# Eight experts in another order: all moved up by one position where neighbours had changed places

## The chip, the cores and the metric

One core of a Trainium2 chip runs the whole program in one launch. The metric is the time of one execution in device microseconds (us), lower is better. The engines are TensorE (PE in the views; PEld is its weight load, which overlaps), VectorE (DVE), ScalarE (ACT), GpSimd (POOL) and SyncE (SP, which here only issues transfers).

## What is computed

Attention with a compressive memory feeds a mixture of experts with one expert per token. There are 2304 tokens of 512 features, 8 experts, and 1024 hidden features in each.

```python
logits = x @ w_gate
expert_idx = np.argmax(logits, axis=1)
...
for e in range(E):
    mask = expert_idx == e
    ...
    h = np.maximum(xe @ w1[e], 0.0)
    ye = h @ w2[e]
    out[mask] = gate_w[mask, None] * ye
```

The inputs come from a seeded generator, so the routing is fixed. It gives experts 0 to 7 these numbers of tokens: 2, 465, 120, 834, 36, 680, 12, 155.

## The kernel before

The first 262 us are the attention stage, with its steps placed by a table of times (`K`), and at its end the routing: each token's expert, its rank within it, and the table `idx` of the tokens in the order in which they are to be worked on. The rest is the expert stage, which this change is about.

The experts are worked on one after another in eight **positions**. `weight_unit` (line 78) says which expert's weights stand at position p: p ^ 1, so 1, 0, 3, 2, 5, 4, 7, 6. `setup` (lines 184 to 186) puts the gate's columns into the same order, so that column p of the logits is that of position p. `Routing.consts` (line 1029) writes the weights `w8` by which a tie goes to the lower expert.

The tokens of a position are cut into blocks of 128. A remainder of 65 to 127 makes one more full block, a remainder of up to 64 a half block (lines 1167 to 1176: counts + 127 and + 63, shifted by 7). The counts reach every engine through the tile `r_cnt` at run time, so each engine runs loops and branches over them (`conv_loops` for ScalarE and VectorE, `turns` for SP, blocks F, H, X, Y, N, Z for TensorE). The first block is done ahead of the loops by straight code; blocks are counted here from that one as 0.

A block on TensorE: 96 products that make the hidden features (line 1581, into `ph`), then the second products into `py` (line 1597 for a full block, line 1594 for a half one, in two column halves). VectorE turns `ph` into `hT` in two parts, hi and lo (lines 1750, 1752). ScalarE moves `py` to `ysb` (lines 1710, 1708), and GpSimd scatters the rows to the output (line 1503). For the next block, GpSimd gathers 128 rows (line 1489), VectorE multiplies them with their gate values into `xn` (lines 1779, 1782), SP issues two transposes into `xB` (line 1410), and VectorE copies that to `xT` (line 1793), which TensorE's next block waits for.

Weights come as fp32, eight units of 512 KB for each position. SP loads them four units (a half) at a time, one half in each turn (line 1383). ScalarE makes the hi part of a unit (line 1271, `conv_hi`), VectorE the lo part (line 1275, `conv_lo`); one half is converted in each block until all are done, halves 0 to 13 for positions 1 to 7. At position e, `conv_loops` first finishes the halves of position e + 1 and then goes on with those of e + 2. Every combination is a copy of the body of its own in the program: `step(e, 0, ...)` for full, `step(e, 1, ...)` for half blocks. In a full block's body VectorE's order is hT of the first half, one conversion, hT of the second half, one conversion, the copy to xT, two conversions. In a half block's body it is both hT, one conversion, the copy to xT, three conversions (`cuts`).

TensorE has three copies of each body, because three sets of converted weights take turns; they stand in the program in this order, each followed by its branches:

```python
for i in range(3):
    with block(f"F{i}"):
        pe_body(rr, i, 0)
...
    with block(f"H{i}"):
        pe_body(rr, i, 1)
```

Position p uses copy p mod 3: F for its full blocks, H for its half block. From F0 the program goes to F0 again (more full blocks), to H0, to F1 or to H1 (line 1656).

Of the kernel before, what the change touches and what calls it, by code (L numbers as in the profile page):

```python
# [76 lines left out]

def weight_unit(w1, w2, p, u):

    e = p ^ 1  # L80
    if u < 4:
        return w1[e, 128 * u:128 * u + 128, :]
    return w2[e, 256 * (u - 4):256 * (u - 4) + 256, :].rearrange("(f p) d -> p f d", p=128)
# [18 lines left out]
def attention(nc, tc, es, q, k, v, M_prev, z_prev, beta, wg, w1, w2, x_dram, logits, mem, rout=None):  # L102
# [44 lines left out]
    for ab in range(2):  # L147
        nc.gpsimd.affine_select(out=maskt[64 * ab:64 * ab + 64], in_=maskt[64 * ab:64 * ab + 64],
                                pattern=[[-1, 64]], compare_op=ALU.is_ge, fill=-1e30, base=0,
                                channel_multiplier=1)  # L150
# [21 lines left out]
    def setup():  # L172
        wg_sb = const.tile([128, 4, 8], F32, name="wg_sb")
        nc.sync.dma_start(out=wg_sb, in_=wg.rearrange("(c p) e -> p c e", p=128))
        bt = const.tile([128, 8], F32, name="bt")
        nc.sync.dma_start(out=bt, in_=beta.rearrange("(o h) -> o h", o=1).to_broadcast([128, 8]))

        gm = const.tile([128, 8], F32, name="gm")
        gl = const.tile([128, 8], F32, name="gl")
        nc.scalar.activation(out=bt, in_=bt, func=AF.Tanh, scale=0.5)  # L180
        nc.vector.tensor_scalar(out=gm, in0=bt, scalar1=0.5 * SX, scalar2=0.5 * SX, op0=ALU.mult, op1=ALU.add)
        nc.vector.tensor_scalar(out=gl, in0=bt, scalar1=-0.5 * SX, scalar2=0.5 * SX, op0=ALU.mult, op1=ALU.add)

        wg_in, wg_sb = wg_sb, const.tile([128, 4, 8], F32, name="wg_sw")
        for i in range(2):
            nc.vector.tensor_copy(out=wg_sb[:, :, i::2], in_=wg_in[:, :, 1 - i::2])
        IW = const.tile([128, 4, 2, 72], F32, name="IW")
        nc.gpsimd.memset(IW, 0.0)
        for hh in range(2):
            r = slice(64 * hh, 64 * hh + 64)  # L190
            nc.vector.tensor_copy(out=IW[r, :, hh, 0:64], in_=ident[r, 64 * hh:64 * hh + 64].unsqueeze(1).to_broadcast([64, 4, 64]))
            nc.vector.tensor_copy(out=IW[r, :, hh, 64:72], in_=wg_sb[r])
        mz = xp.tile([128, 32, 64], F32, tag="xb", name="mz")
        early = xp.tile([128, 512], F32, tag="xt", name="early")
        zt = early[0:32, 256:384].rearrange("p (a d) -> p a d", a=2)
        for hh in range(2):
            nc.sync.dma_start(out=zt[:, hh], in_=z_prev.rearrange("b h d -> (b h) d"))
        mh = const.tile([128, 32, 73], F16, name="mh")
        ml = const.tile([128, 32, 73], F16, name="ml")
        nc.gpsimd.memset(ml[64:128], 0.0)  # L200
        T["gm"] = gm
        mw = early[:, 0:256].rearrange("p (i e) -> p i e", e=8)
        wgp = early[:, 384:512].rearrange("p (c m) -> p c m", c=4)
        nc.gpsimd.memset(wgp, 0.0)
        for hh in range(2):
            nc.vector.tensor_copy(out=wgp[64 * hh:64 * hh + 64, :, 8 * hh:8 * hh + 8], in_=wg_sb[64 * hh:64 * hh + 64])
        mt = xp.tile([128, 32, 64], F32, tag="xb", name="mt2").rearrange("p a d -> p (a d)")
        T.update(IW=IW, gl=gl, mh=mh, ml=ml, mz=mz, mw=mw, zt=zt, wgp=wgp, pws=mt[:, 1024:1536].rearrange("p (b a d) -> p b a d", b=4, a=2),
                 mt=mt[:, 0:1024].rearrange("p (c b d) -> p c b d", c=4, b=4))
# [578 lines left out]
    def wload(e, u):  # L788
        nc.sync.dma_start(out=as_unit(wplace(e, u), u), in_=weight_unit(w1, w2, e, u))
# [116 lines left out]
    at(K["k1"], load, 1, "k")  # L906
    at(K["k1"], load, 1, "q")
    at(K["setup"], setup)
    at(K["v1"], load, 1, "v")
    for i in range(4):  # L910
# [68 lines left out]
NE = 8  # L979
# [9 lines left out]
class Routing:  # L989
# [25 lines left out]
    def consts(s):  # L1015
        V, G, kp = s.nc.vector, s.nc.gpsimd, s.tc.keep_in_program_order
        kp(G.memset(s.tri, 1.0))
        kp(G.affine_select(out=s.tri, in_=s.tri, pattern=[[1, 128]], compare_op=ALU.is_gt, fill=0.0, base=0, channel_multiplier=-1))
        kp(G.memset(s.ones, 1.0))
        kp(G.memset(s.cnt[:, NE:], 0))  # L1020
        kp(G.memset(s.idx[:, NS:NS + 1], 2303))
        kp(G.memset(s.ids[:, NS:NS + 1], 2304))
        ii = s.idx[:, 0:NS]
        it = s.tmp
        kp(G.iota(ii, pattern=[[128, NS]], base=0, channel_multiplier=0))
        kp(V.tensor_scalar(out=s.col, in0=ii, scalar1=BIG, scalar2=None, op0=ALU.add))
        kp(G.iota(it, pattern=[[-1, 128]], base=0, channel_multiplier=0))
        kp(V.tensor_copy(out=s.neg, in_=it))
        kp(G.iota(it[:, 0:NE].rearrange("p (a b) -> p a b", b=2), pattern=[[-2, NE // 2], [1, 2]], base=NE - 1, channel_multiplier=0))
        kp(V.tensor_copy(out=s.w8, in_=it[:, 0:NE]))  # L1030
        kp(G.iota(it[:, NE:2 * NE], pattern=[[128 * NJ, NE]], base=0, channel_multiplier=0))
        kp(V.memset(s.first, 0.0))
        kp(V.memset(s.less, 0.0))
        kp(V.memset(s.less[0:1, 0:1], -128.0))
        kp(V.tensor_copy(out=s.first[0:1], in_=it[0:1, NE:2 * NE]))
        tok = it[:, 16:34]
        for i in range(2):
            kp(G.iota(tok[:, 9 * i:9 * i + 8].rearrange("p (b t) -> p b t", t=4), pattern=[[576, 2], [128, 4]], base=1152 * i - 2304,
                      channel_multiplier=1))
            for a in range(2):  # L1040
                kp(G.iota(tok[64 * a:64 * a + 64, 9 * i + 8:9 * i + 9], pattern=[[0, 1]], base=512 + 576 * (2 * i + a) - 2304, channel_multiplier=1))
        kp(V.tensor_copy(out=s.vals, in_=tok))
# [181 lines left out]
def experts(nc, tc, es, x_dram, mem, rout, w1, w2, out):  # L1224
# [29 lines left out]
    with tc.tile_critical():  # L1254
# [127 lines left out]
        def load(e, u):  # L1382
            SP.dma_start(out=as_unit(stage[e % 2][u], u), in_=weight_unit(w1, w2, e, u)).then_inc(wsem[e % 2][u], 16)
# [457 lines left out]
```

## Time and profile before

| | us |
|---|---|
| median of three runs | 503.66 |
| lowest, highest | 499.33, 504.02 |
| profiled execution, its own time | 500.64 |
| its span, first to last instruction | 498.9 |
| TensorE busy | 462.2 |
| VectorE busy | 356.3 |
| ScalarE busy | 221.7 |
| GpSimd busy | 212.6 |

The mean granted clock of TensorE over the span is 0.98 of full speed. The span and all rows below are of that one profiled execution; its own time is the span and 1.7 us around it. In a row of a timeline, the first figure is the start in us from the span's start, the second the length; a bracket gives the engine's idle time just ahead of it and what ended it. "issue" stands for idle time that ended with nothing the profile shows.

### The profile page before, as it was taken

How to read it: one execution, taken by the hardware profiler on the slowest of the kernel's cores; microseconds unless marked ns; L12 is line 12 of the kernel's file. 1: busy time of each engine (PE TensorE's matmuls, PEld its weight loads, DVE VectorE, ACT ScalarE, POOL GpSimd, SP SyncE). 2: the span in 40 equal slices, each digit the busy share in tenths (PEclk: the TensorE clock that was granted, in tenths of full speed). 3: DMA queues.
4: the chain of work that ended last, by engine and by line, in shares of the span. 5: the costliest groups of instructions: out<-in, count | busy, mean ns of one | idle time of the engine just before them, and what ended most of it. 6: DMA issues, size and time to landing. Idle time of an engine off the chain costs nothing.

```text
span 498.9 us, 14292 instructions
## 1 busy us (share of the span) xinstructions
PE 462.2 (93%) x5269; PEld 316.8 (64%) x5270; DVE 356.3 (71%) x785; ACT 221.7 (44%) x361; POOL 212.6 (43%) x395
## 2 busy tenths in 40 slices
PE   2999799999999989999989996999999999999795
PEld 0555356566666646657656774966777667777774
DVE  2788489787869647999885776898844588743682
ACT  3688465556666564557510443433300333300611
POOL 6567558367748344656231421232232122231132
PEclk9999799999999999999979999899999999999998
DMA  5567979899898989866148999799873459952332
GB/s 118 126 119 159 181 153 163 177 192 232 176 163 163 270 166 184 180 167 218 47 133 286 245 286 281 227 268 333 272 149 97 125 158 346 292 132 76 57 76 70
DMA packets 170106, 90.57 MB, mean 182 GB/s; under 512 B 151471, under 2 KB 152751, under 8 KB 170032
## 3 DMA queue, kind: packets, MB, share of 16 engines
q1 hardware_dynamic: 166192, 77.95, 67.2%
q0 software_dynamic: 3840, 11.80, 7.8%
q8 instruction: 26, 0.43, 0.4%
q14 instruction: 48, 0.39, 0.3%
HBM read 55.35 MB, written 11.60 MB: 134 GB/s over the span
## 4 chain that ended last, share of the span: by engine, by line
PE 60%; DVE 12%; DMA 10%; SPq 8%; issue 5%; ACT 2%; POOL 2%; DVEq 1%; POOLq 0%; ACTq 0%
PE m_ph L1581 17%; PE m_py L1597 13%; PE o L565 7%; PE st L491 5%; DMA m_xB<-m_xn 4%; SPq L275 3%; PE sm L596 3%; PE loc L677 3%; DMA m_xg<-x_scratch,m_ig 2%; PE sn L404 2%; SPq L277 2%; DMA QT<-mem 1%; PE m_py L1594 1%; PE wm L882 1%; DMA mem<-in_v_dram 1%
## 5 line engine op out<-in xcount | busy, mean ns | idle before, releaser
L1581 PE MATMUL m_ph<-m_xT,mem 128*128 128x128 f16 (+1 forms) x1344 | 68.8, 214 | 8.3 <-issue 4.3
L1581 PEld LDWEIGHTS m_ph<-m_xT,mem 128*128 128x128 f16 x1344 | 67.5, 100 | 12.2 <-issue 9.8
L412 DVE TENSOR_REDUCE mt<-sn 128x1 f32<-128x512 f32 (+4 forms) x83 | 54.4, 665 | 13.0 <-PE sn L410 10.7
L510 ACT ACTIVATE aT<-st 128x512 f32<-128x512 f32 x96 | 55.4, 594 | 18.4 <-PE st L491 18.0
L1710 ACT ACTIVATE m_y<-m_py 128x512 f32<-128x512 f32 x17 | 10.2, 597 | 117.0 <-PE m_py L1597 117.0
L495 POOL TENSOR_SCALAR_AFFINE_SELECT aT<-aT 128x128 f32<-128x128 f32 (+2 forms) x160 | 48.4, 320 | 32.3 <-ACT aT L510 30.3
L565 PE MATMUL o<-aT,mem 128*64 128x320 f32 (+4 forms) x320 | 59.2, 433 | 0.0
L1597 PE MATMUL m_py<-mem,m_hT 128*128 128x512 f16 x264 | 58.9, 379 | 0.0
L1750 DVE TENSOR_SCALAR m_hT<-m_ph 128x512 f16<-128x512 f32 (+1 forms) x46 | 29.0, 631 | 40.2 <-PE m_ph L1581 37.8
L1537 POOL COPY m_ig<-r_idx 128x1 int32 x22 | 4.1, 186 | 115.3 <-DVE m_xn L1782 114.3
L491 PE MATMUL st<-mem 128*128 128x64 f16 (+6 forms) x224 | 46.6, 262 | 0.4 <-ACT aL L532 0.2
L491 PEld LDWEIGHTS <-mem 128*128 128x128 f16 (+1 forms) x448 | 33.0, 99 | 16.3 <-issue 4.6
L1597 PEld LDWEIGHTS m_py<-mem,m_hT 128*128 128x128 f16 x264 | 25.3, 98 | 28.3
L491 PE MATMUL st<-QT,mem 66*128 66x64 f16 (+6 forms) x224 | 42.2, 262 | 0.4 <-ACT QT L455 0.4
L1581 PEld LDWEIGHTS m_ph<-m_xT,m_w 128*128 128x128 f16 x768 | 40.9, 98 | 1.8 <-issue 0.4
L1581 PE MATMUL m_ph<-m_xT,m_w 128*128 128x128 f16 (+1 forms) x768 | 41.6, 216 | 0.0
L1597 PE MATMUL m_py<-m_w,m_hT 128*128 128x512 f16 x168 | 37.4, 379 | 0.0
L565 PEld LDWEIGHTS o<-aT,mem 128*64 128x64 f32 x320 | 25.3, 137 | 16.7 <-issue 9.8
L1503 POOL DMA_INDIRECT out_dram<-m_y,m_is x23 | 25.5, 1109 | 20.1 <-POOL m_is L1509 18.0
L404 PE MATMUL sn<-mem 128*128 128x128 f16 (+3 forms) x158 | 31.4, 277 | 1.5 <-DVE mt L412 1.1
L1489 POOL DMA_INDIRECT m_xg<-x_scratch,m_ig x22 | 24.0, 1090 | 17.5 <-POOL m_ig L1537 17.5
L1275 DVE SCALAR_TENSOR_TENSOR mem<-mem,mem 128x1024 f16<-128x1024 f32 x24 | 28.6, 1218 | 2.5 <-ACT mem L1271 2.5
(257 smaller groups left out, 910.3 us busy)
## 6 DMA issues: line engine op xcount, KB each, us to landing
mem<-in_moe_w_dram SPq DMA_DIRECT2D x40, 512.0 KB, 6.0
m_stage<-in_moe_w_dram SPq DMA_DIRECT2D x24, 512.0 KB, 6.6
mem<-in_k_dram SPq DMA_DIRECT2D x32, 128.0 KB, 3.0
mem<-in_q_dram SPq DMA_DIRECT2D x32, 128.0 KB, 2.8
mem<-in_v_dram SPq DMA_DIRECT2D x32, 128.0 KB, 2.7
x_scratch<-xb SPq DMA_DIRECT2D x3, 1152.0 KB, 5.6
mem<-mem SPq DMA_DIRECT2D x6, 288.0 KB, 4.2
x_scratch<-xb SPq DMA_DIRECT2D x1, 864.0 KB, 3.8
```

Of the source, the lines that this page charges most:

```text
L404: nc.tensor.matmul(ps[:, c:c + k1 - k0], QT[:, 5 * hh + t, :], keys(hh)[:, k0:k1], start=(c == 0), stop=(k1 == parts[-1][3] and hh == part ...
L412: nc.vector.reduce_max(out, v, axis=AX.X)
L491: nc.tensor.matmul(ps[:, c:c + n], kk[:, kb, :], qq[:, w:w + n], start=(first and i == 0 and j == 0), stop=(last and i == 1 and j == len(p ...
L495: nc.gpsimd.affine_select(out=ap, in_=ap, pattern=pattern, compare_op=ALU.is_ge, fill=0.0, base=base, channel_multiplier=-1)
L510: nc.scalar.activation(out=a, in_=ps, func=AF.Exp, scale=ESC)
L565: nc.tensor.matmul(o[64 * hh:64 * hh + 64, q0:q0 + n], vv, aa, start=(j == 0), stop=(j == 4), skip_group_check=True)
L1275: V.scalar_tensor_tensor(out=W[e % 3][1][:, u], in0=stage[e % 2][u], scalar=SW, in1=W[e % 3][0][:, u], op0=ALU.mult, op1=ALU.subtract).the ...
L1489: G.indirect_dma_start(out=x.rearrange("p h e -> p (h e)"), out_offset=None, in_=x_dram, in_offset=bass.IndirectOffsetOnAxis(ap=i, axis=0) ...
L1503: G.indirect_dma_start(out=out, out_offset=bass.IndirectOffsetOnAxis(ap=i, axis=0), in_=ysb[:, j], in_offset=None, bounds_check=bound, oob ...
L1581: mm = PE.matmul(ph[i2][:, f, 0:N], w[:, kc, c:c + 128], x[:, j, kc, 0:N], start=(i == 0), stop=(i == 11), skip_group_check=True)
L1597: mm = PE.matmul(py, hh, ww[:, 4 + ff // 2, c:c + 512], start=st, stop=sp_)
L1750: V.tensor_scalar(out=hT[i2][0][:, :, 0:N], in0=ph[i2][:, :, 0:N], scalar1=0.0, scalar2=None, op0=ALU.max).then_inc(S[hi], 1)
```

## The change

Position p gets expert (p + 1) mod 8, so the order is 1, 2, 3, 4, 5, 6, 7, 0. The gate's columns and the tie weights follow. No loop, no body and no queue is touched.

```diff
 def weight_unit(w1, w2, p, u):
 
-    e = p ^ 1
+    e = (p + 1) % 8
...
         wg_in, wg_sb = wg_sb, const.tile([128, 4, 8], F32, name="wg_sw")
-        for i in range(2):
-            nc.vector.tensor_copy(out=wg_sb[:, :, i::2], in_=wg_in[:, :, 1 - i::2])
+        nc.vector.tensor_copy(out=wg_sb[:, :, 0:7], in_=wg_in[:, :, 1:8])
+        nc.vector.tensor_copy(out=wg_sb[:, :, 7], in_=wg_in[:, :, 0])
...
-        kp(G.iota(it[:, 0:NE].rearrange("p (a b) -> p a b", b=2), pattern=[[-2, NE // 2], [1, 2]], base=NE - 1, channel_multiplier=0))
+        kp(G.iota(it[:, 0:NE], pattern=[[-1, NE]], base=NE - 1, channel_multiplier=0))
+        kp(G.iota(it[:, NE - 1:NE], pattern=[[0, 1]], base=NE, channel_multiplier=0))
         kp(V.tensor_copy(out=s.w8, in_=it[:, 0:NE]))
```

What the counts make of it (F a full block, H a half one; position 0 has one more block ahead of the loops):

| position | expert before | tokens | blocks | expert after | tokens | blocks |
|---|---|---|---|---|---|---|
| 0 | 1 | 465 | FFF | 1 | 465 | FFF |
| 1 | 0 | 2 | H | 2 | 120 | F |
| 2 | 3 | 834 | 7 F | 3 | 834 | 7 F |
| 3 | 2 | 120 | F | 4 | 36 | H |
| 4 | 5 | 680 | 5 F, H | 5 | 680 | 5 F, H |
| 5 | 4 | 36 | H | 6 | 12 | H |
| 6 | 7 | 155 | F, H | 7 | 155 | F, H |
| 7 | 6 | 12 | H | 0 | 2 | H |

The bodies stand in the program as before, on every engine; the counts send the engines into others. On TensorE, these are the full body F0 and its branches, and behind it the half body H0, as they stand in the program before (`m_ph` the first products, `m_py` the second, `mem` the converted weights).

```order
L1581 MATMUL m_ph_4111<-m_xT,mem_59 128x128 x48
...
L1597 MATMUL m_py<-mem_59,m_hT_4098 128x512 x8
...
L1682 COMPARE_AND_BRANCH
L1684 COMPARE_AND_BRANCH
...
L1656 UNCONDITIONAL_BRANCH
L1581 MATMUL m_ph_4111<-m_xT,mem_59 128x64 x48
...
L1594 MATMUL m_py<-mem_59,m_hT_4098 64x256 x16
```

Position 3 ran the first of these two and now runs the second; position 1 ran H1 and now runs F1, their copies two bodies further on. So the way through the bodies was F0, H1, F2, F0, F1 and is F0, F1, F2, H0, F1.

On VectorE, at position 1, this is the step that ran before: the half body with the conversions of one half of weights, from behind the branch at line 1348 (`m_w` the converted weights of position 2, `m_stage` the loaded ones).

```order
L1779 TENSOR_SCALAR m_xn_4094<-m_xg_4093 128x512
L1782 SCALAR_TENSOR_TENSOR m_xn_4095<-m_xg_4093,m_xn_4094 128x512
L1750 TENSOR_SCALAR m_hT_4098<-m_ph_4111 128x4x64
...
L1752 SCALAR_TENSOR_TENSOR m_hT_4101<-m_ph_4112,m_hT_4100 128x4x64
L1275 SCALAR_TENSOR_TENSOR m_w_4089<-m_stage_4102,m_w_4089 128x1024
L1793 COPY m_xT<-m_xB 128x1024
L1275 SCALAR_TENSOR_TENSOR m_w_4089<-m_stage_4102,m_w_4089 128x1024 x3
```

In its place the full body with the same four conversions runs, which stands directly behind the branch at line 1343; this is its second part in the program before.

```order
L1750 TENSOR_SCALAR m_hT_4100<-m_ph_4112 128x512
L1752 SCALAR_TENSOR_TENSOR m_hT_4101<-m_ph_4112,m_hT_4100 128x512
L1275 SCALAR_TENSOR_TENSOR m_w_4089<-m_stage_4102,m_w_4089 128x1024
L1793 COPY m_xT<-m_xB 128x1024
L1275 SCALAR_TENSOR_TENSOR m_w_4089<-m_stage_4102,m_w_4089 128x1024 x2
```

At position 3 the same exchange is made the other way round: the full body there is left for a half body, in which two conversions more stand behind the copy and one fewer ahead of it.

On GpSimd the program itself changes, in the constants of the routing (`r_tmp` is the scratch tile of the iotas):

```order
 L1029 IOTA r_tmp 128x8
-L1031 IOTA r_tmp 128x8
-L1038 IOTA r_tmp 128x8
-L1041 IOTA r_tmp 64x1 x2
...
+L1030 IOTA r_tmp 128x1
+L1032 IOTA r_tmp 128x8
+L1039 IOTA r_tmp 128x8
+L1042 IOTA r_tmp 64x1 x2
```

One iota of one column has been added; the others are the same, one line lower.

## Rows read from the trace of the kernel before

**Rows 1.** The page: span, busy time by engine, the chain that ended last.
```profile
span 498.9 us, 14292 instructions
PE 462.2 (93%) x5269; PEld 316.8 (64%) x5270; DVE 356.3 (71%) x785; ACT 221.7 (44%) x361; POOL 212.6 (43%) x395
PE 60%; DVE 12%; DMA 10%; SPq 8%; issue 5%; ACT 2%; POOL 2%; DVEq 1%; POOLq 0%; ACTq 0%
```

**Rows 2.** TensorE's waits from 262 us: who, for whom, us, times, longest.
```profile
PE m_ph L1581 <- issue: 5.8, 2, 4.3
PE m_ph L1581 <- DVE m_xT L1793: 3.9, 3, 3.1
```

**Rows 3.** TensorE's timeline: start, length, line, operation, count, idle time before.
```profile
295.69 5.52 PE L1581 MATMUL m_ph<-m_xT,mem 128*128 128x128 f16 x96 [0.48 <-DVE m_xT L1793]
301.05 5.34 PE L1597 MATMUL m_py<-mem,m_hT 128*128 128x512 f16 x24
310.67 4.51 PE L1581 MATMUL m_ph<-m_xT,mem 128*128 128x64 f16 x96 [4.28 <-issue]
...
317.96 5.52 PE L1581 MATMUL m_ph<-m_xT,m_w 128*128 128x128 f16 x96
...
391.73 5.52 PE L1581 MATMUL m_ph<-m_xT,mem 128*128 128x128 f16 x96
...
402.27 5.52 PE L1581 MATMUL m_ph<-m_xT,mem 128*128 128x128 f16 x96
...
454.97 3.27 PE L1581 MATMUL m_ph<-m_xT,mem 128*128 128x64 f16 x96
...
461.06 2.97 PE L1581 MATMUL m_ph<-m_xT,m_w 128*128 128x64 f16 x96
...
470.05 5.52 PE L1581 MATMUL m_ph<-m_xT,mem 128*128 128x128 f16 x96 [3.10 <-DVE m_xT L1793]
```

**Rows 4.** Stretches: length, busy time of five engines, granted clock, DMA share, GB/s.
```profile
310.67:317.96 7.29, 7.29 (x145) 6.87 (x146) 4.56 (x9) 2.05 (x3) 2.48 (x4) 0.77 0.43 99
...
391.73:402.27 10.54, 10.54 (x121) 7.71 (x120) 6.94 (x9) 4.49 (x5) 2.29 (x3) 1.00 0.83 261
...
454.97:461.06 6.09, 5.95 (x145) 5.29 (x144) 2.03 (x5) 0.60 (x1) 2.29 (x3) 1.00 0.52 136
```

**Rows 5.** VectorE's timeline at position 1.
```profile
311.47 0.48 DVE L1779 TENSOR_SCALAR m_xn<-m_xg 128x512 f16<-128x512 f32 x1 [4.72 <-issue]
```

**Rows 6.** The page: one of two queues of code; packets, MB, share.
```profile
q8 instruction: 26, 0.43, 0.4%
```

**Rows 7.** DMA from 303 to 309 us: the same queue.
```profile
q8 instruction: 1, 0.02, 0.9%
```

**Rows 8.** DMA from 309 to 313 us: the same queue.
```profile
q8 instruction: 1, 0.02, 1.4%
```

**Rows 9.** DMA from 330 to 455 us: all queues that moved anything.
```profile
q1 hardware_dynamic: 19472, 19.01, 54.7%
q0 software_dynamic: 2000, 6.55, 16.4%
q14 instruction: 15, 0.12, 0.4%
```

**Rows 10.** ScalarE's timeline at position 3.
```profile
395.59 3.90 ACT L1271 ACTIVATE m_w<-mem 128x1024 f16<-128x1024 f32 x4 [2.92 <-issue]
```

**Rows 11.** VectorE's timeline at position 3: a conversion and the copy.
```profile
396.68 1.23 DVE L1275 SCALAR_TENSOR_TENSOR m_w<-mem,m_w 128x1024 f16<-128x1024 f32 x1 [0.65 <-ACT m_w L1271]
...
400.28 0.42 DVE L1793 COPY m_xT<-m_xB 128x1024 f16<-128x1024 f16 x1
```

**Rows 12.** ScalarE's timeline at position 5.
```profile
466.37 3.90 ACT L1271 ACTIVATE mem<-mem 128x1024 f16<-128x1024 f32 x4 [4.20 <-issue]
```

**Rows 13.** GpSimd's timeline: two iotas of the routing's constants.
```profile
120.23 0.15 POOL L1029 IOTA r_tmp<- 128x8 int32 x1 [0.16 <-DVE r_neg L1028]
120.34 0.14 POOL L1031 IOTA r_tmp<- 128x8 int32 x1
```

## The prediction

> **What bounds the kernel now.** I read the page first. TensorE is busy for 462.2 of the 498.9 us of the span, and holds most of the chain that ended last [rows 1]. So what counts is where TensorE stands still, or runs something longer than it must. The change touches what runs after about 262 us, the expert stage, so the second view is the list of TensorE's waits there: 5.8 us put down to "issue" (one wait of 4.3) and 3.9 us to VectorE's copy into xT (one of 3.1) [rows 2]. The reader is to see that almost everything is in two places. The third view, TensorE's timeline, says where [rows 3]. A full block (128 rows) takes 10.54 us from its start to the next one's (391.73 to 402.27). A half block (64 rows) takes 6.09 us (454.97 to 461.06). Block 4, the only block of position 1, is a half one: the block before ends at 301.05 + 5.34 = 306.39, block 4 starts at 310.67 after 4.28 us of "issue", and the next starts at 317.96. So position 1 costs 11.57 us, more than a full block, with a clock of 0.77 in its running part, where the other blocks have 1.00 [rows 4]. Position 3 is one full block, 10.54 us.
>
> **The change part by part.** The weights and the gate columns are reordered the same way, so each token still meets its own expert. Only the positions differ. The reference's routing gives experts 0 to 7 these numbers of tokens: 2, 465, 120, 834, 36, 680, 12, 155. The order before is 1 0 3 2 5 4 7 6, the order after 1 2 3 4 5 6 7 0. A remainder over 64 takes a full block, a smaller one a half block. Positions 0, 2, 4 and 6 keep experts 1, 3, 5 and 7 with their blocks. Position 1 goes from 2 tokens to 120, so from half to full; position 3 from 120 to 36, so from full to half; positions 5 and 7 stay half (36 to 12, 12 to 2). There are as many blocks of each kind as before, and by lines 1342 to 1375 the same half of weights is converted in the same block of the row. Per block the gather and the two transposes are the same, and so are four weight loads a turn on SP's queue. Scattered rows only change places. One full and one half block trade places, and that is all.
>
> *Place A, position 1.* Before: 11.57 us. After: a full block, 10.54 us, plus what TensorE then waits. Why did it stand before? Neither data nor weights: VectorE too stood 4.72 us for "issue" and went on only at 311.47 [rows 5], so two engines at once waited for nothing that a semaphore shows. Both had left the code they had been in. The queue that carries 16 KB packets of code [rows 6] moved one in 303 to 309 us and one in 309 to 313 [rows 7, 8]. I read these as TensorE's: from F0 (the full body in use) it had jumped over H0 and F1 into H1. Between 330 and 455 us that queue moved none [rows 9], while TensorE went from F2 to F0 at 391.73 and to F1 at 402.27, F1 for the first time, with no idle time [rows 3]. So the code of F1 had been fetched by 330. After the change TensorE goes from F0 to F1, the nearer body, which an earlier fetch in sequence may hold already, and then over H1 to F2. I take the 4.28 us as gone.
>
> [...]
>
> VectorE may still lose time there. Its full step stands right behind the branch at line 1343, the half step behind two more, so its 4.72 us may go as well. If they stay, its first step of block 4 begins at 311.47, some 2 us later hT is ready, and TensorE, done with its first products at 306.39 + 5.52 = 311.9, waits about 1.6 us. The bounds of the extra wait are 0 and 1.6 us; I take 0.5, next to the 0.48 us wait for xT at 295.69 [rows 3]. Gain at A: 11.57 - 11.04 = 0.53 us; 1.03 at best.
>
> *Place B, position 3.* Before: 10.54 us. After: 6.09 us and a wait. This half block carries four conversions. VectorE's half step runs relu, relu, one conversion, the copy into xT, three conversions; so the copy, for which TensorE's next block waits, stands behind a conversion that needs ScalarE. Queued behind that are VectorE's three other conversions and its next gather product, and then SP's transposes of it. In the block as it is, ScalarE stood 2.92 us for "issue" and converted from 395.59 [rows 10]; VectorE converted from 396.68 for 1.23 [rows 11], so the copy (0.42) could end at 398.33. The half block would end at 391.73 + 6.09 = 397.82, and TensorE would wait 0.5 us. VectorE too enters another step; I take 0.9 for both. The bounds are 0 and 3.10 us, the wait at 470.05 behind the one half block that now carries conversions [rows 3], where ScalarE had stood 4.20 us [rows 12]. The full block's slack now hides ScalarE's delay, and the half block takes away that cover. Gain at B: 10.54 - 6.99 = 3.55 us, between 1.35 and 4.45.
>
> *Setup.* The two copies of the gate columns stay two. GpSimd issues one more iota, of one column; iotas there start 0.11 us apart [rows 13]. VectorE's copy into w8 stands behind it, and the attention stage behind that. TensorE's work covers it; without that cover, 0.1 us. I charge 0.1, between 0 and 0.3.
>
> *Sum.* 0.53 + 3.55 - 0.1 = 4.0 us less. The profiled execution took 500.64 us, 3.0 less than the median of 503.66; against itself the sum gives 496.7, against the median 499.7. The four times I have spread over 4.7 us, so I apply the sum to their mean, 501.9: **497.9 us**.
>
> **The rivals.** *Both places come out clean* (0 extra at A and B): 1.03 + 4.45 - 0.1 = 5.4 us less, 496.5 us. For it: single half blocks before a block without conversions run on without a wait (454.97 to 461.06). Against it: ScalarE's 2.92 us at just this place. *The code wait moves.* TensorE leaves F1 over H1 for F2, which was entered from H1, its neighbour, before. If F2's code is fetched only then, 4.28 us come back: A costs 10.54 + 4.28 = 14.82, a loss of 3.25, and with B nothing is won: 501.7 us. For it: the jump is as long as that over H0. [...] *Place B is not won.* If ScalarE's delay is 4.20 as at position 5, or the transposes land late, the wait is 3.1 us or more, B gives 1.35 or less, and the total is 500.1 us. Against it: only one conversion stands ahead of the copy. *Slower.* Each body entered for the first time out of order pays for its code, so that F1 and F2 both do: 2 x 4.28, and the slow clock behind an idle spell (4.51 against 2.97 us for the same products, rows 3), 1.54. A is then 10.54 + 8.56 + 1.54 = 20.64, 9.1 us worse; with B and the setup, 5.6 us slower: 507.5 us. The kernel as a whole is slower from 4.5 us of idle time around block 4 on (1.03 + 3.55 - 0.1). Against it: F1's first entry at 402.27 had no wait, and no packet of code came just ahead of it. That the change does nothing is excluded by the counts: two blocks change kind.
>
> **How the numbers follow.** Forecast 0.50, clean 0.17, code wait moves 0.14, B not won 0.12, slower 0.07. One per cent is 5.0 us, about what a measurement of this kernel can tell from no change. The forecast lies 1 us inside it, the clean case just past it, and the scatter of the times (2.6 us from mean to lowest) moves both: faster 0.28 (0.12 of clean, 0.16 of the forecast), slower 0.09 (0.06 of its rival, 0.03 of scatter from the two cases without a gain), same 0.63. The range runs from 494 (the clean case less the 2.6 us) to 503 (the moved code wait and 1.3 of scatter); it leaves out the slower case and thin tails, under 0.2 in all.
>
> **What would show it.** Right: block 4 is full, starts within 0.5 us of the block before it, and its clock is 1.00; block 12 is half, at about 391, and the block behind it starts 6 to 7.5 us later, after a wait for VectorE's copy; all other blocks keep 10.54 and 6.1 us. Wrong: an "issue" wait of TensorE ahead of block 4 or 5, with 16 KB packets of code in it; hT late in block 4; over 2 us of wait for xT after block 12; or a change before 262 us, where I expect none over 0.3 us.

## The result, and the profile after

The changed kernel takes 498.38 us (median of 12 executions, 493.57 to 504.91), the kernel before 502.50 (12, 499.33 to 505.55). The ratio is 0.987, interval 0.983 to 0.991. It leaves out the four longest executions of the changed kernel, as more than 1.5 per cent above its fastest, and none of the kernel before; by the means of all 12 it is 0.992. Both kernels were measured twice more (experiments 1 and 2):

| comparison | changed kernel, mean | before, mean | difference | ratio as above, with its interval |
|---|---|---|---|---|
| first | 498.62 (12) | 502.61 (12) | -4.0 | 0.987, 0.983 to 0.991 |
| second | 497.87 (12) | 500.33 (41) | -2.5 | 0.995, 0.990 to 0.999 |
| third | 497.84 (12) | 500.66 (35) | -2.8 | 0.997, 0.993 to 1.001 |

The counts in brackets are executions. The ratios of the means, of all executions, are 0.992, 0.995 and 0.994. Taken together, the change wins about 3 us, 0.6 per cent. The forecast was 4.0 us less and 497.9 us. The total came out; its parts did not, as the profile shows.

The page of the changed kernel (span, busy time, the chain that ended last, as in [rows 1]):

```profile
span 498.9 us, 14289 instructions
PE 462.2 (93%) x5269; PEld 316.1 (63%) x5270; DVE 355.5 (71%) x785; ACT 221.2 (44%) x361; POOL 215.7 (43%) x396
PE 67%; DVE 11%; DMA 7%; issue 5%; SPq 3%; ACT 3%; POOL 2%; DVEq 1%; POOLq 0%; ACTq 0%
```

This profiled execution took 500.61 us, as long as the one of before (500.64), so the page alone says that nothing happened. TensorE's timeline says that much happened and evened out. Its answer to [rows 3], the places A and B and the block at 470 us:

```profile
301.81 5.34 PE L1598 MATMUL m_py<-mem,m_hT 128*128 128x512 f16 x24
310.37 6.93 PE L1582 MATMUL m_ph<-m_xT,mem 128*128 128x128 f16 x96 [3.21 <-issue]
317.13 5.34 PE L1598 MATMUL m_py<-mem,m_hT 128*128 128x512 f16 x24
322.90 5.52 PE L1582 MATMUL m_ph<-m_xT,m_w 128*128 128x128 f16 x96 [0.42 <-DVE m_w L1276]
...
396.68 2.96 PE L1582 MATMUL m_ph<-m_xT,mem 128*128 128x64 f16 x96
399.57 2.91 PE L1595 MATMUL m_py<-mem,m_hT 128*64 128x256 f16 x48
403.59 5.52 PE L1582 MATMUL m_ph<-m_xT,mem 128*128 128x128 f16 x96 [1.11 <-DVE m_xT L1794]
...
470.12 5.52 PE L1582 MATMUL m_ph<-m_xT,mem 128*128 128x128 f16 x96 [1.81 <-DVE m_xT L1794]
```

Place A: block 3 ends at 301.81 + 5.34 = 307.15 and position 2 starts at 322.90, so position 1 costs 15.75 us. It was 11.57 before, and 11.04 were forecast. The wait for "issue" is still there, 3.21 us, now ahead of F1, and the products behind it run slowly (6.93 instead of 5.52 us; the clock of the stretch is 0.88, below). That is what the prediction named as its first sign of being wrong, and one 16 KB packet of code came in the wait (one between 307 and 308 us; the page has 26 of them with 0.43 MB). Place B: 403.59 - 396.68 = 6.91 us where there were 10.54; 6.99 were forecast.

```profile
310.37:322.90 12.53, 12.11 (x120) 9.05 (x121) 7.63 (x9) 2.68 (x4) 1.51 (x3) 0.88 0.80 222
396.68:403.59 6.91, 5.80 (x146) 5.34 (x144) 4.55 (x9) 3.40 (x4) 3.00 (x4) 1.00 0.40 88
```

Place A loses 4.18 us and place B wins 3.63. The rest is waits that came out shorter in this execution: block 2 takes 10.54 us and not 11.19, since the 0.48 us wait of [rows 3] is absent, and from block 19's start to block 20's it is 7.63 and not 8.99 (a wait of 1.81 and not 3.10). With 0.06 elsewhere, the stretch from the first expert block (264.38) to the end is 4.18 - 3.63 - 0.65 - 1.36 + 0.06 = 1.40 us shorter, and the attention stage ahead of it happened to be 1.40 longer.

There is a view that the prediction did not use: all instructions of one line. The jump into another body is a branch of TensorE's sequencer (PEldq in this view; duration in ns as min/median/max). Line 1655 sends the changed kernel from F0 to F1, line 1656 sent the kernel before from F0 to H1. The one of each near 304 us, of the changed kernel and then of the kernel before:

```profile
L1655 PEldq COMPARE_BRANCH  x1: 6077/6077/6077, 304.1 to 304.1; - x1
```
```profile
L1656 PEldq COMPARE_BRANCH  x1: 6614/6614/6614, 303.9 to 303.9; - x1
```

Of the seven branches of line 1655 in this profile five take 67 to 225 ns, and the seven of line 1654 in the profile before take 67 to 233 ns; the jump to F2 near 319.5 us takes 3.27 us. The two above took 6.08 and 6.61 us. The sequencer reached them ahead of the products: 304.1 against block 3's end at 307.15, 3.0 us of lead (2.5 before). What TensorE stood still was about the jump's price less the lead: 6.08 - 3.0 = 3.1 (3.21 seen), and 6.61 - 2.5 = 4.1 (4.28 seen).

### The profile page after: what moved, and what is told of

It reads as the page before. It is cut to its first block, busy times and chain, and to the rows that moved or that the text cites. A ratio compares the mean times of both kernels' runs of the same rounds, so it can differ in the third digit from the quotient of the medians.

```text
span 498.9 us, 14289 instructions
## 1 busy us (share of the span) xinstructions
PE 462.2 (93%) x5269; PEld 316.1 (63%) x5270; DVE 355.5 (71%) x785; ACT 221.2 (44%) x361; POOL 215.7 (43%) x396
## 4 chain that ended last, share of the span: by engine, by line
PE 67%; DVE 11%; DMA 7%; issue 5%; SPq 3%; ACT 3%; POOL 2%; DVEq 1%; POOLq 0%; ACTq 0%
PE m_ph L1582 19%; PE m_py L1598 16%; PE o L565 7%; PE st L491 6%; PE sm L596 3%; PE loc L677 3%; PE sn L404 2%; DMA mem<-in_moe_w_dram 2%; SPq L275 1%; DMA QT<-mem 1%; DMA mem<-mem 1%; DVE mt L412 1%; DVE m_w L1276 1%; SPq L277 1%; PE wm L882 1%
## 5 line engine op out<-in xcount | busy, mean ns | idle before, releaser
L495 POOL TENSOR_SCALAR_AFFINE_SELECT aT<-aT 128x128 f32<-128x128 f32 (+2 forms) x160 | 49.6, 327 | 34.4 <-ACT aT L510 32.2
L1504 POOL DMA_INDIRECT out_dram<-m_y,m_is x23 | 30.1, 1310 | 19.9 <-POOL m_is L1510 11.3
L1753 DVE SCALAR_TENSOR_TENSOR m_hT<-m_ph,m_hT 128x512 f16<-128x512 f32 (+1 forms) x46 | 29.1, 633 | 1.6
```

The lines of the kernel that those rows point to most:

```text
L495: nc.gpsimd.affine_select(out=ap, in_=ap, pattern=pattern, compare_op=ALU.is_ge, fill=0.0, base=base, channel_multiplier=-1)
L1504: G.indirect_dma_start(out=out, out_offset=bass.IndirectOffsetOnAxis(ap=i, axis=0), in_=ysb[:, j], in_offset=None, bounds_check=bound, oob ...
L1753: V.scalar_tensor_tensor(out=hT[i2][1][:, :, 0:N], in0=ph[i2][:, :, 0:N], scalar=0.0, in1=hT[i2][0][:, :, 0:N], op0=ALU.max, op1=ALU.subtr ...
```

## The experiments

**1. The changed kernel twice more.** No edit.

> The changed kernel once more, to see what one execution differs from the next in. In its first profile TensorE waited 3.21 us for issue ahead of block 4 (307.15 to 310.37), where it enters F1 for the first time, and two 16 KB packets of code moved just then (307.75 and 311.08). Theory, code by chance: whether F1's code has come before it is entered differs between executions of one program; an execution with an earlier code packet, near 297 us as in the kernel before, would show no wait there and be about 5 us shorter from 262 us on (3.2 of wait, 1.4 of slow clock, 0.4 behind it). Rival, fixed cost: the change of position from 0 to 1 itself (its counts, its weights) makes the wait; then it stands in every profile with 3 to 4 us, and what differs between executions lies before 262 us, in the attention stage. Ratio to the kernel before 0.983 to 0.991 by either.

The second profile repeats the first: a jump of 6.66 us, a wait of 3.80, a first part of block 4 of 8.04 us, and 235.21 us from the first expert block to the end.

```profile
307.65 8.04 PE L1582 MATMUL m_ph<-m_xT,mem 128*128 128x128 f16 x96 [3.80 <-issue]
```
```profile
L1655 PEldq COMPARE_BRANCH  x1: 6657/6657/6657, 300.8 to 300.8; - x1
```

The ratio, 0.995, lies outside the 0.983 to 0.991 that both theories expected. The third time:

> The changed kernel a third time, to settle how large its gain is: by its two comparisons it is 1.3 and 0.5 per cent, while the stretch from the first expert block to the end is 1.4 us (0.3 per cent) shorter than that of the kernel before in each pair of profiles (235.92 to 234.52, 236.59 to 235.21). Theory, the places alone (A lost, B won): that stretch takes 234 to 236 us again, TensorE's wait ahead of block 4 is 3 to 4 us, the jump ahead of it takes 6 to 7 us, and the ratio is 0.992 to 0.998. Rival, most executions of the changed kernel have no wait there, and the two profiles were the exceptions: a stretch near 230 us without a wait, ratio 0.985 to 0.990.

There, TensorE goes from F0 to F1 without a wait, and the branch takes 0.34 us. TensorE's timeline of this third profile, and the same branch:

```profile
299.52 5.34 PE L1598 MATMUL m_py<-mem,m_hT 128*128 128x512 f16 x24
304.70 5.52 PE L1582 MATMUL m_ph<-m_xT,mem 128*128 128x128 f16 x96
310.06 5.34 PE L1598 MATMUL m_py<-mem,m_hT 128*128 128x512 f16 x24
316.19 5.52 PE L1582 MATMUL m_ph<-m_xT,m_w 128*128 128x128 f16 x96 [0.79 <-DVE m_w L1276]
```
```profile
L1655 PEldq COMPARE_BRANCH  x1: 338/338/338, 301.8 to 301.8; - x1
```

Position 1 costs 11.33 us there (304.86 to 316.19), and the stretch from the first expert block is 229.50 us. One program, one input, and 4.4 and 5.5 us between its executions at one branch. What differs ahead of it is a packet of code: in the DMA view from 276 to 300 us, the queue of the 16 KB packets moved one in the third profile, and none in the first two.

```profile
q8 instruction: 1, 0.02, 0.3%
```

Neither expectation was right as a whole: two of three profiles have the wait, one has not.

**2. The kernel before twice more.** No edit.

> The kernel before once more. Both theories expect a ratio of 1.00. Theory, code by chance: the wait of 4.28 us ahead of block 4 may be of another size, since H1 is entered over H0 and F1, but it is there, with a 16 KB packet of code in it; the packet at 296.88 us need not be there. Rival, fixed cost: 4.28 us again within 0.3.

> The kernel before a third time, for the same. The wait ahead of block 4 is 4 to 5.5 us, the jump ahead of it takes 6.5 to 8 us, the stretch from the first expert block to the end 235.5 to 237 us, the ratio 0.998 to 1.004: how far it is from 1.000 is how far a comparison of these sizes can err here. No theory expects another time.

The jump to H1 took 7.99 and 7.33 us, the wait was 5.46 and 4.60 us: it is in all three profiles, and not within 0.3 us of 4.28. Times stand at 1.004 (0.999 to 1.009) and 1.003 (0.999 to 1.006) of the kernel before itself, so a comparison here can err by 0.3 to 0.4 per cent. In the third profile something came that the first two do not have: the first entry of F1, at position 4, cost a jump too. With it, its slow products and a jump of 1.53 us at block 19, the stretch from the first expert block came to 240.72 us, and not to the 235.5 to 237 expected.

```profile
L1654 PEldq COMPARE_BRANCH  x1: 4517/4517/4517, 400.6 to 400.6; - x1
```
```profile
405.25 7.15 PE L1581 MATMUL m_ph<-m_xT,mem 128*128 128x128 f16 x96 [2.33 <-issue]
```

That branch took 0.21 us in the other two. And here too it goes with the early packet of code: the first two moved one 16 KB packet between 276 and 300 us, the third none. Over the six profiles of the two kernels, F1's first entry was free in the three with that packet and cost 4.5 to 6.7 us in the three without.

**3. TensorE's bodies in the order in which the changed kernel enters them.** One branch has its two ways exchanged, and the program then lays the bodies out as F0, F1, F2, H0, H1, H2.

```diff
-                PE.br_lt(rr.regs[0, 1], lim[i][1], on_true=f"H{i}", on_false=f"Y{i}")
+                PE.br_eq(rr.regs[0, 1], lim[i][1], on_true=f"Y{i}", on_false=f"H{i}")
```

> The changed kernel, with TensorE's six bodies in another order in the program: F0, F1, F2, H0, H1, H2, each with its branches (one branch has its two ways exchanged), which is the order in which the changed kernel enters them for the first time. The same blocks, products and waits. Theory, code: F1 now stands directly behind F0 and its branches, so its code comes in sequence while F0 runs, and the wait ahead of block 4 falls from 3.21 us to under 0.5; block 4 starts and runs at full clock, 10.5 to 11 us instead of 15.75, about 4.5 us less from 262 us on, a ratio near 0.978 to 0.982 to the kernel before. F2 behind F1, and H0 behind F2, come in sequence too. Rival, fixed cost of the change of position: the wait stays at 3 to 4 us and the ratio at 0.987.

> The changed kernel with TensorE's bodies in the order F0, F1, F2, H0, H1, H2 a second time. Theory, code: with F1 behind F0 no execution has the jump's price (6.1 and 6.7 us in two of the three profiles of the changed kernel, hidden in the third), so no wait ahead of block 4 again, a stretch of 229 to 230 us from the first expert block to the end as in the changed kernel's profile without the wait (229.50), times between 493 and 500 us, ratio 0.987 to 0.994. Rival, the absence of the wait in the two profiles of this order was the same luck as in that one profile: the wait of 3 to 4 us is back, with a jump of 6 us or more, and the times spread to 505.

In both, block 4 follows block 3 without a wait and at full clock. TensorE's timeline of the first run, and its branch:

```profile
300.74 5.34 PE L1598 MATMUL m_py<-mem,m_hT 128*128 128x512 f16 x24
305.92 5.52 PE L1582 MATMUL m_ph<-m_xT,mem 128*128 128x128 f16 x96
...
316.46 5.52 PE L1582 MATMUL m_ph<-m_xT,m_w 128*128 128x128 f16 x96
```
```profile
L1655 PEldq COMPARE_BRANCH  x1: 214/214/214, 303.1 to 303.1; - x1
```

That F1's code came in sequence while F0 ran, as the theory has it, no view shows; what is measured is that the wait is gone. No branch of TensorE in the expert stage took more than 0.4 us in either run, and from block 3's start to block 5's it is 21.08 us against 26.45 in the first profile of the changed kernel. The medians are 495.17 (ratio 0.993, 0.990 to 0.996) and 497.22 us (ratio 0.991, 0.987 to 0.994). This version is faster than the kernel before in both comparisons, though less than the 0.978 to 0.982 expected of the first, and 2.2 us faster than the changed kernel where both ran together (means 495.7 and 497.9). The gain over the changed kernel is smaller than its 5 us at block 4. Some executions of that kernel do without the wait as well, and place B gives some of it back: with this order of bodies it takes 8.19 and 8.33 us, with the other 6.91 to 7.68. One rival is left: all three profiles of this order (the third is that of experiment 6) have the early packet between 276 and 300 us, with which F1's first entry was free in the changed kernel too. That the layout and not this luck took the wait away speaks from the narrow times (493.18 to 499.49 and 496.08 to 498.22 us) and is not shown for F1; experiment 5 shows it for H1, without that packet. The second run's stretch is 232.40 us, not 229 to 230: it has waits of 2.50 and 2.38 us for xT ahead of blocks 13 and 20 (see experiment 6).

**4. The same order of bodies in the kernel before.** The same edit, without the change.

> The kernel before with the same other order of TensorE's bodies, F0, F1, F2, H0, H1, H2. It enters them in the order F0, H1, F2, F0, F1. Theory, code: H1 is entered over F1, F2 and H0, so it waits as before (4 to 5 us); F2 is now entered by a jump backwards over F1's branches and may wait too, up to 4 us more; the layout alone wins nothing, ratio 1.000 to 1.008. Rival, fixed cost: ratio 1.00 and a wait of 4.28 us at block 4 alone. [...]

```profile
307.74 5.28 PE L1581 MATMUL m_ph<-m_xT,mem 128*128 128x64 f16 x96 [3.65 <-issue]
312.95 2.92 PE L1594 MATMUL m_py<-mem,m_hT 128*64 128x256 f16 x48
319.88 7.09 PE L1581 MATMUL m_ph<-m_xT,m_w 128*128 128x128 f16 x96 [4.01 <-issue]
```

Both jumps are paid, F0 to H1 with 6.38 us and H1 back to F2 with 4.84. It is slower, 1.011 (1.006 to 1.017), a little beyond what was expected; by the means of all executions it is 1.008. So this order does not help by itself, whatever is entered: it helped the kernel that enters the bodies in it.

**5. The bodies of the kernel before in its own order.** Here a second branch is exchanged, in the code behind F0 and H0 only (`i` numbers the copies of the bodies), and the layout is F0, H1, F2, H0, F1, H2.

```diff
             with block("N" + t):
-                PE.br_lt(rr.regs[0, 1], lim[k][0], on_true=f"F{k}", on_false="Z" + t)
+                if i == 0:
+                    PE.br_eq(rr.regs[0, 1], lim[k][0], on_true="Z" + t, on_false=f"F{k}")
+                else:
+                    PE.br_lt(rr.regs[0, 1], lim[k][0], on_true=f"F{k}", on_false="Z" + t)
```

> The kernel before, with TensorE's bodies in the order F0, H1, F2, H0, F1, H2 (two branches with their ways exchanged): H1 stands directly behind F0, and F2 behind H1, as the kernel before enters them first. F1 is first entered from F0 over three bodies. Theory, code: no wait ahead of block 4 (4.28 and 5.46 us in the two profiles before) and none ahead of block 5; block 4 runs at full clock in about 6.1 to 6.5 us instead of 7.3 to 8.5. In their place a wait of 3 to 4 us for issue ahead of block 13, where F1 is entered for the first time (none there before), with about 1.5 to 2.5 us of slow clock. In all 0 to 3 us less, ratio 0.994 to 1.000. Rival, the change of position from 0 to 1 makes the wait: it stays at block 4 and nothing happens at block 13.

TensorE enters H1 without a wait, in a profile without an early packet. But then it stands 3.53 us for hT, and two blocks on 2.93 us for xT:

```profile
304.23 2.96 PE L1581 MATMUL m_ph<-m_xT,mem 128*128 128x64 f16 x96
310.73 4.20 PE L1594 MATMUL m_py<-mem,m_hT 128*64 128x256 f16 x48 [3.53 <-DVE m_hT L1753]
...
328.50 5.52 PE L1581 MATMUL m_ph<-m_xT,m_w 128*128 128x128 f16 x96 [2.93 <-DVE m_xT L1796]
```

VectorE's timeline shows why at the first:

```profile
308.89 0.49 DVE L1782 TENSOR_SCALAR m_xn<-m_xg 128x512 f16<-128x512 f32 x1 [4.13 <-issue]
```

VectorE had its own wait there all the time (4.72 us in [rows 5]), beside TensorE's; with TensorE's gone it ends last. That VectorE too waits for code is a reading and not shown: no instruction of its sequencer took over 1.3 us in any of these profiles (0.55 and 0.79 us at most in the expert stage of the first profiles of the two kernels), so the wait stands in no branch, as TensorE's does. The wait of F1 that was expected at block 13 did not come. Ratio 0.999 (0.995 to 1.002): one engine's fetch was taken away, the next engine's wait stood behind it.

**6. Place B: the copy ahead of the conversions.** On top of experiment 3, VectorE's half-block step copies into xT before it converts anything.

```diff
-cuts=((1, 2), (0, 1))
+cuts=((1, 2), (0, 0))
```

> The changed kernel with TensorE's bodies in the order F0, F1, F2, H0, H1, H2 as before in this study, and in VectorE's half-block step the copy into xT ahead of the conversions instead of behind the first (one number of the table). Theory for place B: the half block at position 3 is followed by a wait of 2.35 us (1.11 and 1.88 in the two profiles of the changed kernel) because the copy stands behind a conversion for which ScalarE is late; with the copy ahead of it the wait of block 13 falls to 0.3 us or less, and that of the first full block of position 6 (0.45 to 3.10) too; 2 to 3 us less than the 495.2 of that order of bodies alone, ratio to the kernel before about 0.987. Rival: the wait is for the transposes (the DMA into xB), which land late; then it stays over 1 us, put down to the DMA or to VectorE behind it, and the time stays within 1 us.

The wait of block 13 stays, 2.56 us, and so does that at position 6, 2.76. In VectorE's timeline the copy is now ahead of the conversions, and still late:

```profile
388.89 0.49 DVE L1780 TENSOR_SCALAR m_xn<-m_xg 128x512 f16<-128x512 f32 x1 [3.96 <-issue]
...
395.95 0.43 DVE L1794 COPY m_xT<-m_xB 128x1024 f16<-128x1024 f16 x1 [3.90 <-DMA m_xB<-m_xn]
```

It waits for the transposes, which start late because VectorE reached its product xn late, after 3.96 us of "issue" at the entry of the half-block step. The rival is right for this order of bodies. Behind both waits hT then came late too, by 0.89 us, and the stretch from the first expert block is 234.37 us (229.08 and 232.40 without the edit). Ratio 0.993 (0.990 to 0.996), as without the edit.

**7. Place B alone.** The experts stand as 1 0 3 4 5 2 7 6, with the gate columns and the tie weights to match; the bodies stand as before.

```diff
-    e = p ^ 1
+    e = (1, 0, 3, 4, 5, 2, 7, 6)[p]
```

> Place B alone: the order 1 0 3 4 5 2 7 6. Position 1 keeps the half block of expert 0, so TensorE enters H1 as before; position 3 gets the half block of expert 4 and position 5 the full block of expert 2. The bodies stand as in the kernel before. Theory, by places: position 1 costs what it cost (11.6 to 14.0 us from block 3's end to block 5), position 3 falls from 10.54 to 6.9 to 8.2, position 5 goes from 6.1 plus a wait of 0.5 to 3.1 behind it to 10.54 with none: 0.5 to 2.3 us less than before in all, ratio 0.995 to 0.999; the way through TensorE's bodies is F0, H1, F2, H0, F1. Rival, the code wait is moved by any change of order: a wait for issue of 3 us or more ahead of block 12 or 13, where H0 is now entered for the first time from F2 by a jump backwards; then 1 to 5 us slower than before, ratio 1.002 to 1.010.

No code wait at blocks 12 and 13. Position 1 costs its jump of 6.90 us as before. The half block at position 3 takes 8.17 us, but the block behind it 12.00, since it runs slowly after its wait:

```profile
398.76 6.99 PE L1583 MATMUL m_ph<-m_xT,mem 128*128 128x128 f16 x96 [2.38 <-DVE m_xT L1795]
```

Position 5's full block takes 10.55 us with no wait behind it. Ratio 0.994 (0.991 to 0.997), against an expected 0.995 to 0.999. So the time fell without any change at position 1, but the profile does not show where: its stretch from the first expert block is 236.58 us, against 235.92, 236.59 and 240.72 in the three of the kernel before. What the half block at position 3 won there, its slow successor and the full block at position 5 took back. That the half block alone is the gain is not shown.

**8. Light weight loads.** What the jump costs is either the fetch itself or the traffic that it meets. These two versions leave out three quarters of the rows of the weights of positions 3 to 7; there is one execution of each.

```diff
-            SP.dma_start(out=as_unit(stage[e % 2][u], u), in_=weight_unit(w1, w2, e, u)).then_inc(wsem[e % 2][u], 16)
+            n = 128 if e < 3 else 32
+            SP.dma_start(out=as_unit(stage[e % 2][u], u)[0:n], in_=weight_unit(w1, w2, e, u)[0:n]).then_inc(wsem[e % 2][u], 16)
```

> The changed kernel with the weights of positions 3 to 7 loaded in a quarter of their rows only (32 of 128 partitions; the rest of each unit keeps the values of an earlier expert), so that the weight loads put a quarter of the bytes on the queues from block 2 on. Everything else runs as it did. Theory, fixed price: the wait ahead of block 4 is the time from the jump to the code's use, mostly outside the queues, since the packet itself took 0.9 to 1.0 us in both profiles; it stays at 2.8 to 4 us. Rival, the price is the traffic: code packets queue behind the weights' packets, and the wait falls to 1.5 us or less.

> The kernel before with the weights of positions 3 to 7 loaded in a quarter of their rows only (32 of 128 partitions; the rest keeps older values), as in the run of the changed kernel with light loads, where the jump to F1 took 3.5 instead of 6.1 to 6.7 us and the wait of TensorE went. Theory, the price of the jump is the traffic: the jump to H1 takes 3.3 to 4.5 us instead of 6.6 to 8.0, and TensorE, whose sequencer runs 2.5 to 3 us ahead, waits 0.3 to 1.5 us instead of 4.3 to 5.5; VectorE's wait for issue at position 1 (4.72 us, 4.13 in another run) shrinks by 1 us or more as well. Rival: H1 lies farther than F1 and its code must be fetched whatever the traffic; the wait stays above 3 us.

The jump is there in both, at about half its price. Of the changed kernel with light loads, the branch near 301 us and block 4:

```profile
L1656 PEldq COMPARE_BRANCH  x1: 3535/3535/3535, 300.7 to 300.7; - x1
```
```profile
304.36 5.52 PE L1583 MATMUL m_ph<-m_xT,mem 128*128 128x128 f16 x96 [0.67 <-DVE m_w L1276]
```

And of the kernel before with light loads, the jump to H1:

```profile
L1657 PEldq COMPARE_BRANCH  x1: 3748/3748/3748, 304.1 to 304.1; - x1
```

6.08 and 6.66 us become 3.54; 6.61 to 7.99 become 3.75. The sequencer's lead of 2.5 to 3 us then hides nearly all of it: TensorE waits 0.67 and 1.02 us, and the profile puts both down to VectorE's conversions. The theory of a fixed price falls, that of the traffic stands. The DMA views from 303 to 307 us, where the changed kernel's packet is waited for, show what is ahead of it; first the changed kernel, then the same with light loads, whose packet had come by then:

```profile
DMA packets 349, 1.29 MB, mean 323 GB/s; under 512 B 35, under 2 KB 35, under 8 KB 348
q1 hardware_dynamic: 339, 1.25, 93.6%
```
```profile
DMA packets 509, 0.17 MB, mean 41 GB/s; under 512 B 504, under 2 KB 504, under 8 KB 507
q1 hardware_dynamic: 504, 0.13, 26.7%
```

With the queues 94 per cent busy the code packet is seen only 3 to 4 us after the jump began (none between 304 and 307 us, one between 307 and 308); with light loads it is seen between 301 and 302, at most 1.3 us after it. All nine paid jumps out of F0 at position 1 in these profiles, seven of them with full loads, divide in the same way. From the branch's start to the packet's it is 3.6 to 5.5 us with full loads and 1.1 and 1.2 with light ones; from the packet's start to the branch's end it is 2.3 to 2.7 us in all nine. So what differs from jump to jump is how long the packet is waited for. The price is 3.54 and 3.75 us with light loads, which is not without traffic (in the kernel before with light loads q1 is 31.1 and q0 18.6 per cent busy from 303 to 307 us, around its jump), and 2.5 to 4.2 us more with full ones. VectorE's wait at position 1 shrank as well, from 4.72 to 0.51 us in the kernel before with light loads.

## Why the prediction was right in its total, and where it was wrong

**What bounds the kernel.** Right: TensorE's waits at two places are what moved. That the 4.28 us were a fetch of code, which the prediction read from 16 KB packets, is shown by the branch itself (6.61 us, with one 16 KB packet in it, between 308 and 309 us) and by experiment 5, in which another layout takes the wait away with the same products; for F1 in the changed kernel it is shown by its branches (6.08 and 6.66 us).

**Place A.** Wrong, and this is the step that failed: "I take the 4.28 us as gone." It rested on F1's code having been "fetched by 330", which the rows show, and on "an earlier fetch in sequence may hold already", which they do not. Held by 330 is not held by 304, when the sequencer needed it. Whether it was held differs between executions: free in one profile of three, 6.08 and 6.66 us in the others. The term was a gain of 0.53 us; the three profiles of the changed kernel have 15.75, 16.86 and 11.33 us at position 1, those of the kernel before 11.57, 13.96 and 12.93. On average that is a loss of 1.8 us; against the mean of 12.82 before, two profiles lose 2.9 and 4.0 and one wins 1.5. The size of the rival "the code wait moves" (a loss of 3.25) was near the two losses (4.2 in the first pair), but its place was not: F1 itself waited, not F2. The jump to F2 took 3.27, 2.16 and 3.65 us in the three profiles, about what the lead hides. The "slower" rival was right in part, that a body entered for the first time out of order pays, and its counterargument wrong: F1's first entry at 402.27 was free in that execution, which had the early packet, and in the third profile of the kernel before it was not.

The first entries out of F0 at position 1 that were paid are F0 to H1 in all three profiles of the kernel before and, in two of the three of the changed kernel, F0 to F1, 6.1 to 8.0 us each. How much code is held at a time, no run here shows.

**The slow clock.** Forecast 1.00 in block 4, measured 0.88 in the first profile. Behind a wait of 3.21 us the first products took 1.41 us more, behind 3.80 us 2.52 more. This part of the price stood only in the "slower" rival. All nine code waits of 2.3 us and more in these profiles have slow products behind them. Waits for xT of 2.35 to 3.10 us did not always: six were followed by first products at 5.52 us and four by 6.99 to 7.15.

**VectorE at place A.** Its 4.72 us went, as the branch at line 1343 suggested: in the first profile it starts at 307.08, right behind its conversion, with no idle time.

**Place B.** Right in size: 6.91, 7.68 and 7.34 us against 6.99 forecast. The cause is the forecast one in the first profile: ScalarE starts converting at 400.79, the copy waits for one conversion, block 13 for the copy. In the second profile VectorE's entry ended last, by 0.48 us (in the third by 0.18): the chain goes from its branch at line 1358 (2.28 us to the next instruction) to xn, to the transposes and the copy.

```profile
392.51 0.06 DVEq L1358
392.56 2.28 issue
394.84 0.04 DVEq L1306
...
397.48 4.02 DMA m_xB<-m_xn
...
401.59 0.44 DVE m_xT L1794
```

The prediction held the two together in its 0.9 us ("VectorE too enters another step") and its 3.1 us bound. VectorE's wait at the entry of the half step is there in all three profiles (3.97, 3.99 and 4.01 us, against 1.42 ahead of the full step in the kernel before). Experiment 6 shows that with VectorE late, the conversion ahead of the copy does not matter.

**Setup.** Too small to see, as forecast. The first expert block starts at 264.38, 261.09 and 262.10 us in the three profiles of the changed kernel and at 262.98, 262.31 and 261.98 before: 0.1 us apart in the mean, with 3.3 us of scatter.

**The total.** 4.0 us less were forecast; 4.0, 2.5 and 2.8 were measured. Place B's gain is there every time (7.31 us in the mean of the three profiles, 3.2 less than 10.54); place A, which was to add half a microsecond, takes most of it or all back in two profiles and adds to it in the third. The kernel before has a chance price of its own that the sum did not hold: F1's first entry, which the change moves from position 4 to position 1, cost 4.1 us at position 4 in one of its three profiles. In the mean of the three profiles of each kernel place A loses 1.8 us, place B wins 3.2, F1's entry at position 4 wins 1.4, and other waits win 1.9 (they lie between 0.5 and 3.1 us at position 6 alone); that is 4.7 us, more than the times show over all executions. So the forecast time of 497.9 us was met by a sum with a wrong term in it, helped by entries and waits that the sum held constant: that the totals agree so closely is luck.

## What to carry to other kernels

Where control flow picks among long bodies of code, look at the branches themselves, line by line: the jumps of 6.08 and 6.61 us are there in plain numbers, and what TensorE lost by them, 3.21 and 4.28 us, was about that price less the lead of its sequencer (3.0 and 2.5 us). Code that was fetched by some time says nothing of an earlier one, and a free first entry in one profile can be luck (F1's was free in three of six profiles), so look at several. With the bodies laid out in the order of their first entries the wait was gone in both kernels here, and time with it in the changed one (2.2 us); in the kernel before, another engine's wait stood behind it. A first entry out of order cost most where the queues were full of weight loads: 6.1 to 8.0 us at position 1, against 3.54 and 3.75 with a quarter of the rows.

## What the runs showed of the hardware that was not expected

At position 1 a jump out of F0 to code not yet held took 6.1 to 8.0 us under full weight loads (the weight queue was 94 per cent busy in the view above), and 3.54 and 3.75 us with a quarter of the rows. The one at position 4, in the third profile of the kernel before, took 4.5 us. The code packet is one of 16 KB (26 of them move 0.43 MB on the page of either kernel). At position 1, from its start to the end of the branch it is 2.3 to 2.7 us in either case; the rest is the time until it starts.

In some executions of one program one more 16 KB packet of code came between 276 and 300 us. In the six profiles of the two kernels F1's first entry was free when it had come, and cost a jump when it had not. What makes it come stays open, and that it carries F1's code is not shown. Of three more profiles with the same order of bodies, experiment 7 and the changed kernel with light loads fit this, and one goes against it: the kernel before with light loads had that packet and still paid 3.8 us at F1's first entry. So the packet does not always carry the same code, or it is not always kept.

Clearing one engine's code wait laid bare the wait of another at the same place: TensorE's went in experiment 5, and VectorE's 4.13 us took its place.
